# Decode attention beside a gated MLP on one core: three groups of wo behind the last V, a projection in four column tiles, and two K loads left whole

## The chip, the cores and the metric

The kernel runs on one core of one Trainium2 chip. The metric is the device time of that core in microseconds (us). "Span" is the profile's time from the first to the last instruction, some 1.8 us shorter than the device time.

## The reference

Four sequences, one new token each, 32 heads of 128, a cache of 4096 positions. Attention over the cache, a small gated MLP and the residual are summed.

```python
q = (xn @ wq)                                  # (4, 32, 1, 128)
scores = einsum('bhqd,bhkd->bhqk', q, k_cache) * 128 ** -0.5
o = einsum('bhqk,bhkd->bhqd', softmax(scores), v_cache)
attention = o.reshape(4, 1, 4096) @ wo         # wo: (4096, 640)
return x + attention + mlp(xn)                 # xn = layernorm(x)
```

k_cache and v_cache hold 134 MB each in bfloat16; everything else is 14 MB.

## The kernel before

Work is cut into 16 units: four groups of eight heads by four sequences. Each unit has a K and a V of 8.39 MB (64 KB in each of 128 partitions). They are loaded in the order K0 K1 K2 K3 V0 K4 V1 K5 V2 and so on into a ring of five slots; a unit takes two slots, so a load waits until the unit that lay there has been used.

```python
place = {("k", 0): 3, ("k", 1): 0, ("k", 2): 2, ("k", 3): 0}   # first of two slots
for u in range(B, NU):
    place[("k", u)] = 1 if u % 2 == 0 else 0
for u in range(NU):
    place[("v", u)] = 3
...
cuts = {("k", u): (0, T // 2, T) for u in range(B - 1)}        # loads in halves
...
for g in range(NG):
    cuts[("k", B * g + B - 1)] = (0, T // 2, T)
```

For each K unit, VectorE (DVE) transposes eight pieces and TensorE (PE) multiplies them with q. After the fourth unit of a group comes the softmax; then Zb is filled with the probabilities, per sequence, and 64 matmuls with V run in four column tiles (rows 0, 32, 64, 96 of PSUM).

```python
def z_fill(g, b):                       # eight of these on ACT for every V unit
    ... nc.scalar.activation(out=Zb[b % 2][...], in_=src, func=ACT.Copy, scale=MkE[...])

def emit_proj(g, cs=range(HG)):         # 8 chunks, two halves of the 640 columns
    oT = state[("oT", g)]
    for c in cs:
        for hf in range(NH):
            nc.tensor.matmul(proj[32 * hf:32 * hf + B, 0:NO2], lhsT=oT[:, c, :],
                             rhs=wo_t[g][:, c, hf * NO2:(hf + 1) * NO2], ...)
...
emit_proj(NG - 2, range(0, 4))
emit_sel(NG - 1)
emit_proj(NG - 2, range(4, HG))
emit_oT(NG - 1)                         # the attention result of the last group
emit_proj(NG - 1)
o_bf = const.tile([64, NO2], BF16)
nc.vector.tensor_copy(out=o_bf[:], in_=proj[:, 0:NO2])
```

The results of a V unit's four tiles are summed into R. When a group is done, the selection (emit_sel) takes each head's row out of R and divides it by the softmax's sum (om), emit_oT turns the result into oT, and emit_proj multiplies oT with the group's part of wo.

The wo of groups 0 and 1 is loaded in the middle of the stream, that of groups 2 and 3 behind the last V.

Of the kernel before, what the change touches and what calls it, by code (L numbers as in the profile page):

```python
# [8 lines left out]
ACT = mybir.ActivationFunctionType  # L9
ALU = mybir.AluOpType  # L10
AX = mybir.AxisListType
F32 = mybir.dt.float32
BF16 = mybir.dt.bfloat16
# [3 lines left out]
def kernel(  # L17
# [19 lines left out]
    nc = tc.nc  # L37
    P = 128
    B, Sq, D = A_x.shape
# [3 lines left out]
    HG = 8  # L43
    HP = 4
    NE = HG // HP
    M = P // HG
    T = Sk // M
# [4 lines left out]
    NG = H // HG  # L52
    NU = NG * B
# [5 lines left out]
    NOUT = A_wo.shape[1]  # L59
    NH = 2  # L60
    NO2 = NOUT // NH
    scale = float(Dh) ** -0.5
    eps = 1e-5

    const = ctx.enter_context(tc.tile_pool(name="const", bufs=1))
    small = ctx.enter_context(tc.tile_pool(name="small", bufs=2))
# [5 lines left out]
    ps_j = ctx.enter_context(tc.tile_pool(name="ps_j", bufs=1, space=bass.MemoryType.PSUM))  # L72
# [11 lines left out]
    def at_slot(i, n, off=0):  # L84
        return kv[:, i * SL + off:i * SL + off + n]
# [20 lines left out]
    w_out = at_slot(2, FC * NOUT, n_in).rearrange("p (c n) -> p c n", c=FC)  # L106
# [18 lines left out]
        place[("v", u)] = 3  # L125
    place[("v", NU - 3)] = 1
    place[("v", NU - 1)] = 0
    first = {}
    cuts = {("k", u): (0, T // 2, T) for u in range(B - 1)}
    cuts[("v", NU - 1)] = (0, 128, 192, 240, T)  # L130
    for g in range(NG):
        cuts[("k", B * g + B - 1)] = (0, T // 2, T)
    for u in range(B, NU):
        if ("k", u) not in cuts:
            first[u] = u % 2

    def unit(item):
        return at_slot(place[item], 2 * SL)
# [10 lines left out]


    wo_q = A_wo.rearrange("(g p c) n -> g p c n", p=P, c=HG)
    wo_t = [at_slot(3 if g == NG - 2 else 2, HG * NOUT).rearrange("p (c n) -> p c n", c=HG) for g in range(NG)]

    def load_wo(g, c_cuts=(0, HG)):
        for c0, c1 in zip(c_cuts[:-1], c_cuts[1:]):
            nc.sync.dma_start(out=wo_t[g][:, c0:c1, :], in_=wo_q[g][:, c0:c1, :])
# [65 lines left out]
    MkE = const.tile([P, NE], F32)  # L222
# [13 lines left out]
    Zb = []  # L236
# [3 lines left out]
        Zb.append(zt)  # L240


    proj = ps_j.tile([64, 512], F32)



# [1 line left out]
    for hf in range(2):  # L248
        for c in range(DC):
            for j in range(NG):  # L250
                n0 = j * HG * Dh + hf * 512
                nc.tensor.matmul(q4_ps[32 * j:32 * j + 32, hf * 512:hf * 512 + 512], lhsT=xnT[:, c, :],  # L252
                                 rhs=wq[:, c, n0:n0 + 512], start=(c == 0), stop=(c == DC - 1))
# [3 lines left out]
    for r in range(HP):  # L257
        op = nc.vector.tensor_copy if r < 2 else nc.scalar.copy
# [6 lines left out]
    for h in range(HG):  # L265
        for kw in range(4):
            nc.tensor.matmul(q3_ps[:, kw, h, :], lhsT=q4[:, h, kw].rearrange("p r j -> p (r j)"),
                             rhs=SelJ[:].rearrange("p j b -> p (j b)"), start=True, stop=True)
# [5 lines left out]
    for part in range(2):  # L274
        for fc in range(FC):
            n = P if fc < FC - 1 else FL
            f0 = part * Fh
            for c in range(DC):
                if fc < FC - 1:
                    w = w_in[:, c, f0:f0 + nf].rearrange("p (f a) -> p a f", a=FC - 1)[:, fc, :]  # L280
                else:
                    w = w_in[:, c, f0 + nf:f0 + Fh]
                nc.tensor.matmul(zT_ps[:n, part, fc, :], lhsT=w,
                                 rhs=xnT[:, c, 0:B], start=(c == 0), stop=(c == DC - 1))
    zT = const.tile([P, 2, FC, B], F32)
    nc.vector.memset(zT[:], 0.0)
    uT = const.tile([P, FC, 32], BF16)
# [43 lines left out]

    for fc in range(FC):
        n = P if fc < FC - 1 else FL
        nb = B if fc else 32
        for hf in range(NH):
            nc.tensor.matmul(proj[32 * hf:32 * hf + nb, 0:NO2], lhsT=uT[:n, fc, 0:nb],
                             rhs=w_out[:n, fc, hf * NO2:(hf + 1) * NO2], start=(fc == 0), stop=False)


    def fill_qz(g):  # L340
# [50 lines left out]
    def z_fill(g, b):  # L391
        xd = state[("xd", g)]
        for hp in range(HP):
            r0 = 32 * hp
            src = xd[r0:r0 + 32, C2 * b:C2 * b + C2].rearrange("p x q (y c) -> p (x q y) c", c=4)
            for e in range(NE):
                nc.scalar.activation(out=Zb[b % 2][r0:r0 + 32, :, NE * hp + e, :], in_=src, func=ACT.Copy,  # L397
                                     scale=MkE[r0:r0 + 32, e:e + 1])

    def softmax(g):  # L400
        negmax = softmax_max(g)
        S_ps = state.pop(("S", g))
        p_bf = ppool.tile([P, TC, NE, M], BF16, tag="p", name="p")
        rowsum = small.tile([P, NE], F32, tag="rowsum")
        for e in range(NE):
            nc.scalar.activation(out=p_bf[:, :, e, :], in_=S_ps[:, e], func=ACT.Exp, bias=negmax[:, e:e + 1], scale=scale,  # L406
                                 accum_out=rowsum[:, e:e + 1])

        pT = ppool.tile([P, TC, HP, B * C2], BF16, tag="p", name="pT")
        nc.vector.transpose(pT[:].rearrange("p t h x -> p (t h x)"), p_bf[:].rearrange("p t e m -> p (t e m)"))  # L410

        xd = small.tile([P, B * C2, 4, TC], BF16, tag="xd", name="xd", bufs=1)
        state[("xd", g)] = xd
        for hp in range(HP):
            for q in range(4):
                op = nc.vector.tensor_copy if q < 2 else nc.scalar.copy
                op(out=xd[32 * hp:32 * hp + 32, :, q, :], in_=pT[32 * q:32 * q + 32, :, hp, :].rearrange("p t x -> p x t"))  # L417
        z_fill(g, 0)
        z_fill(g, 1)
        cs = misc_ps([G, 1], F32)  # L420
        for e in range(NE):
            nc.tensor.matmul(cs[:], lhsT=SelPe[:, e].rearrange("p h e b -> p (h e b)"), rhs=rowsum[:, e:e + 1],  # L422
                             start=(e == 0), stop=(e == NE - 1))
        rinv = small.tile([G, 1], F32, tag="rinv")
        nc.vector.reciprocal(out=rinv[:], in_=cs[:])
        state[("rinv", g)] = rinv
# [20 lines left out]
    def emit_sel(g):  # L447

        oh = misc_ps([G, Dh], F32)
        for b in range(B):  # L450
            nc.tensor.matmul(oh[:], lhsT=SelR[:, b].rearrange("p h b -> p (h b)"), rhs=state["R"][:, b, :],  # L451
                             start=(b == 0), stop=(b == B - 1))
        om = ppool.tile([G, HG, Dh], BF16, tag="p", name="om")
        nc.vector.scalar_tensor_tensor(out=om[:], in0=oh[:, None, :].to_broadcast((G, HG, Dh)),  # L454
                                       scalar=state.pop(("rinv", g))[:, 0:1],
                                       in1=MkH[:, :, None].to_broadcast((G, HG, Dh)), op0=ALU.mult, op1=ALU.mult)
        state[("om", g)] = om

    def emit_oT(g):
        om = state.pop(("om", g))[:].rearrange("p h (q c) -> p c h q", c=HG)  # L460
        oT_ps = misc_ps([P, HG, B], F32)
        for c in range(HG):
            nc.tensor.matmul(oT_ps[:, c, :], lhsT=om[:, c, :, :], rhs=B32[:], start=True, stop=True)
        oT = small.tile([P, HG, B], BF16, tag="oT")
        nc.vector.tensor_copy(out=oT[:], in_=oT_ps[:])
        state[("oT", g)] = oT

    def emit_proj(g, cs=range(HG)):
        oT = state[("oT", g)]
        for c in cs:  # L470
            for hf in range(NH):
                nc.tensor.matmul(proj[32 * hf:32 * hf + B, 0:NO2], lhsT=oT[:, c, :],  # L472
                                 rhs=wo_t[g][:, c, hf * NO2:(hf + 1) * NO2],
                                 start=False, stop=(g == NG - 1 and c == HG - 1))

    fill_qz(0)
    for i, item in enumerate(seq):
        if i + 1 < len(seq):
            key, u = seq[i + 1]
            if u == NU - 2 and key == "v":  # L480
                nc.sync.dma_start(out=x_res[0:32:4, :], in_=x_flat.rearrange("b (h n) -> (b h) n", h=NH))
            load_unit(seq[i + 1])
            if key == "k" and 2 * B - 1 <= u < NU - 1 and u % B == B - 1:
                load_wo(u // B - 1)
        else:
            load_wo(NG - 2, (0, 4, 8))
            load_wo(NG - 1, (0, 4, 6, 7, 8))
        key, u = item
        g, b = divmod(u, B)
        if key == "k":  # L490
            done = b == B - 1 and g > 0
            for k in range(8):
                emit_K(u, k)
                if done and k == 1:
                    emit_sel(g - 1)
                if done and k == 2:
                    emit_oT(g - 1)
                if done and k == 5 and g < NG - 1:
                    emit_proj(g - 1)
            if b == B - 1:  # L500
                if g < NG - 1:
                    fill_qz(g + 1)
                softmax(g)
        else:
            emit_V(u)
            if u == NU - 2:
                for hf in range(NH):
                    nc.tensor.matmul(proj[32 * hf:32 * hf + B, 0:NO2], lhsT=ident_bf[:32, 4 * hf:32:8], rhs=x_res[:],
                                     start=False, stop=False)
    emit_proj(NG - 2, range(0, 4))  # L510
    emit_sel(NG - 1)
    emit_proj(NG - 2, range(4, HG))
    emit_oT(NG - 1)
    emit_proj(NG - 1)

    o_bf = const.tile([64, NO2], BF16)
    nc.vector.tensor_copy(out=o_bf[:], in_=proj[:, 0:NO2])
    nc.sync.dma_start(out=out_flat[:, 0:NO2], in_=o_bf[0:B, :])
    nc.scalar.dma_start(out=out_flat[:, NO2:NOUT], in_=o_bf[32:32 + B, :])

# [28 lines left out]
```

## Time and profile before

| | before |
|---|---|
| device time, median | 666.86 us (666.03 to 666.89, 6 runs) |
| span of the trace | 665.0 us |
| DVE busy | 353.5 us |
| PE busy | 294.0 us |
| K, V and weights read | 282.25 MB |
| last landing of wo, issue of the output | 660.29, 662.43 us |

The prediction shows the page's shares and slices and the chain over the tail. Two lines of the order of DMA issues follow, and the two landings behind them. The first column is the start in us, the second the length; square brackets give the idle time before the group and what ended it.

```profile
111.56 0.33 SPq L148 DMA_DIRECT2D kv<-in_A_k_cache_dram  x1
133.49 0.33 SPq L148 DMA_DIRECT2D kv<-in_A_v_cache_dram  x1
```

These are K4 and V1. From the same timeline of the kernel before, DVE's first work on K4, and PE's work on V0 and V1:

```profile
141.37 17.66 DVE L356 STREAM_TRANSPOSE kT<-kv 128x2048 f32<-128x2048 f32 x8 [6.37 <-DMA kv<-in_A_k_cache_dram]
...
128.35 5.09 PE L434 MATMUL O<-kv,Zb 128*32 128x512 bf16 x64 [9.77 <-ACT Zb L397]
...
160.74 3.64 PE L434 MATMUL O<-kv,Zb 128*32 128x512 bf16 x64 [0.53 <-DMA kv<-in_A_v_cache_dram]
```

K4 is transposed from 141.37, V1 multiplied from 160.74, and both waited for a DMA: their starts tell when the loads landed. One unit of 8.39 MB lies between them, 19.4 us.

### The profile page before, as it was taken

To read this page: it belongs to the slowest core of one execution; us is meant where nothing else is said; L and a number is where in the kernel's file an instruction comes from. 1 tells how busy PE (TensorE), PEld (TensorE's weight loads), DVE (VectorE), ACT (ScalarE), POOL (GpSimd) and SP (SyncE) were. 2 spreads that over 40 slices of the span, in tenths; PEclk is the share of its full clock that TensorE was granted. 3 is DMA by queue.
4 is the path that set the end of the run, shared out by engine and by line. 5 is a ranking of instruction groups with operands and counts; after the bars stand their busy time and mean duration, and the time that the engine had idled before them with its cause. 6 is when DMAs were issued, how large, how long until landed. Compare 5 with 4: busy or idle time off the path is not lost.

```text
span 665.0 us, 5565 instructions
## 1 busy us (share of the span) xinstructions
PE 294.0 (44%) x2366; PEld 111.6 (17%) x2366; DVE 353.5 (53%) x319; ACT 91.3 (14%) x189; POOL 6.2 (1%) x24
## 2 busy tenths in 40 slices
PE   0566655336052546235335155532705344524365
PEld 0321211112011122011112022210201112111122
DVE  5389997256180849409155286734619074950002
ACT  0300000821100000540200000081020000045200
POOL 0000000000000000000000000000000000000000
PEclk9988788569597697668859596866868769766665
DMA  9999999999999999999999999999999999999995
GB/s 372 424 440 425 426 441 444 438 431 439 434 418 439 434 413 455 434 427 438 419 434 439 434 418 421 452 442 434 427 426 431 438 439 412 464 418 423 429 415 219
DMA packets 7812, 282.60 MB, mean 425 GB/s; under 512 B 888, under 2 KB 1260, under 8 KB 2028
## 3 DMA queue, kind: packets, MB, share of 16 engines
q1 hardware_dynamic: 7772, 282.25, 98.6%
q8 instruction: 18, 0.29, 0.2%
q14 instruction: 6, 0.05, 0.0%
q10 hardware_dynamic: 16, 0.01, 0.0%
HBM read 282.25 MB, written 0.01 MB: 424 GB/s over the span
## 4 chain that ended last, share of the span: by engine, by line
DMA 74%; DVE 10%; issue 10%; PE 3%; ACT 2%; DVEq 0%; SPq 0%; ACTq 0%
DMA kv<-in_A_k_cache_dram 65%; DVE kT L356 9%; DMA kv<-in_A_v_cache_dram 4%; DMA kv<-in_A_wo_dram 3%; DMA kv<-in_A_wq_dram 2%; PE O L434 1%; PE q L252 1%; ACT xd L417 1%; PE proj L472 1%; ACT Zb L397 0%; DVE kv L260 0%; PE S L367 0%; ACT kv L260 0%; ACT p L406 0%; DVE om L454 0%
## 5 line engine op out<-in xcount | busy, mean ns | idle before, releaser
L356 DVE STREAM_TRANSPOSE kT<-kv 128x2048 f32<-128x2048 f32 x128 | 283.4, 2277 | 125.7 <-DMA kv<-in_A_k_cache_dram 125.7
L367 PE MATMUL S<-kT,QZ 128*32 128x512 bf16 x1024 | 185.7, 495 | 232.2 <-DVE kT L356 232.2
L367 PEld LDWEIGHTS <-QZ 128*32 128x32 bf16 x1024 | 59.9, 110 | 351.7 <-issue 330.1
L434 PE MATMUL O<-kv,Zb 128*32 128x512 bf16 x1024 | 75.2, 457 | 66.2 <-ACT Zb L397 39.1
L441 DVE TENSOR_SCALAR R<-O,Mk 128x128 f32<-128x128 f32 x16 | 5.6, 351 | 138.0 <-PE O L434 138.0
L397 ACT ACTIVATE Zb<-xd,MkE 32x256 bf16<-32x256 bf16 x128 | 57.7, 497 | 106.5 <-PE O L434 105.1
L406 ACT ACTIVATE p<-S,negmax 128x512 bf16<-128x512 f32 x8 | 5.4, 683 | 395.1 <-DVE negmax L388 395.1
L434 PEld LDWEIGHTS <-Zb 128*32 128x32 bf16 x1024 | 32.9, 112 | 106.8 <-issue 52.9
L417 ACT COPY xd<-pT 32x256 bf16<-32x256 bf16 x32 | 19.6, 613 | 5.7 <-DVE pT L410 5.2
L443 DVE SCALAR_TENSOR_TENSOR R<-O,Mk,R 128x128 f32<-128x128 f32 x48 | 16.8, 351 | 1.7
L451 PE MATMUL misc<-R,SelR 128*32 128x128 f32 x32 | 6.6, 290 | 24.4 <-DVE R L443 24.4
L417 DVE COPY xd<-pT 32x256 bf16<-32x256 bf16 x32 | 11.7, 364 | 0.6
L472 PE MATMUL proj<-kv,oT 128*4 128x320 bf16 x64 | 9.2, 456 | 1.2 <-DMA kv<-in_A_wo_dram 1.0
L343 POOL COPY QZ<-q 32x32 bf16<-32x32 bf16 x16 | 5.1, 318 | 421.9 <-PE S L367 394.9
L410 DVE STREAM_TRANSPOSE pT<-p 128x1024 bf16<-128x1024 bf16 x4 | 5.0, 1245 | 6.3 <-ACT p L406 6.3
L374 DVE TENSOR_REDUCE m<-S 128x2 f32<-128x1024 f32 x4 | 4.9, 1225 | 5.9 <-PE S L367 5.9
L451 PEld LDWEIGHTS misc<-R,SelR 128*32 128x32 f32 x32 | 2.4, 111 | 31.6 <-DVE R L443 22.7
L260 DVE CAST kv<-q 128x512 bf16<-128x512 f32 x4 | 2.5, 682 | 9.4 <-PE q L252 9.4
L252 PE MATMUL q<-kv,xnT 128*32 128x512 bf16 x40 | 4.5, 629 | 5.1 <-DMA kv<-in_A_wq_dram 5.1
L379 PE MATMUL misc<-dg,ones_f 128*128 128x256 f32 x8 | 3.2, 487 | 7.6 <-DVE dg L376 7.6
L454 DVE SCALAR_TENSOR_TENSOR om<-misc,rinv,MkH 32x1024 bf16<-32x1024 f32 x4 | 5.1, 1272 | 2.6 <-PE misc L451 2.6
L422 PE MATMUL misc<-rowsum,SelPe 128*32 128x1 f32 x16 | 2.1, 200 | 9.0 <-ACT p L406 9.0
(92 smaller groups left out, 60.7 us busy)
## 6 DMA issues: line engine op xcount, KB each, us to landing
kv<-in_A_k_cache_dram SPq DMA_DIRECT2D x14, 4096.0 KB, 30.8
kv<-in_A_wq_dram SPq DMA_DIRECT2D x1, 5120.0 KB, 15.4
kv<-in_A_v_cache_dram SPq DMA_DIRECT2D x1, 4096.0 KB
kv<-in_A_wo_dram SPq DMA_DIRECT2D x2, 1280.0 KB
kv<-in_B_w_in_dram SPq DMA_DIRECT2D x1, 2160.0 KB
kv<-in_A_v_cache_dram SPq DMA_DIRECT2D x1, 2048.0 KB, 33.3
kv<-in_A_wo_dram SPq DMA_DIRECT2D x3, 640.0 KB, 20.0
kv<-in_A_v_cache_dram SPq DMA_DIRECT2D x1, 1536.0 KB
```

The lines of the kernel that those rows point to most:

```text
L252: nc.tensor.matmul(q4_ps[32 * j:32 * j + 32, hf * 512:hf * 512 + 512], lhsT=xnT[:, c, :], rhs=wq[:, c, n0:n0 + 512], start=(c == 0), stop= ...
L343: nc.gpsimd.tensor_copy(out=QZ[r0:r0 + 32, :, :, :, 8 + 8 * hp], in_=q3[r0:r0 + 32, :, NE * hp:NE * hp + NE, g * B:g * B + B].rearrange("p ...
L356: nc.vector.transpose(kT[:].rearrange("p (t r) -> p t r", r=32), kw)
L367: nc.tensor.matmul(S_ps[32 * q:32 * q + 32, e], lhsT=QZ[:, b, 2 * kh + w, e, w0:w0 + 32], rhs=kb[:, i, :, e, :, w], start=(b == 0 and k < ...
L397: nc.scalar.activation(out=Zb[b % 2][r0:r0 + 32, :, NE * hp + e, :], in_=src, func=ACT.Copy, scale=MkE[r0:r0 + 32, e:e + 1])
L406: nc.scalar.activation(out=p_bf[:, :, e, :], in_=S_ps[:, e], func=ACT.Exp, bias=negmax[:, e:e + 1], scale=scale, accum_out=rowsum[:, e:e + 1])
L417: op(out=xd[32 * hp:32 * hp + 32, :, q, :], in_=pT[32 * q:32 * q + 32, :, hp, :].rearrange("p t x -> p x t"))
L434: nc.tensor.matmul(O_ps[32 * q:32 * q + 32, :, :], lhsT=Zb[b % 2][:, w].rearrange("p h c -> p (h c)"), rhs=vv[:, w * 4 * Dh:(w + 1) * 4 * ...
L441: nc.vector.tensor_scalar(out=R, in0=O_ps[:, 0, :], scalar1=Mk4[:, 0:1], scalar2=None, op0=ALU.mult)
L443: nc.vector.scalar_tensor_tensor(out=R, in0=O_ps[:, c, :], scalar=Mk4[:, c:c + 1], in1=R, op0=ALU.mult, op1=ALU.add)
L451: nc.tensor.matmul(oh[:], lhsT=SelR[:, b].rearrange("p h b -> p (h b)"), rhs=state["R"][:, b, :], start=(b == 0), stop=(b == B - 1))
L472: nc.tensor.matmul(proj[32 * hf:32 * hf + B, 0:NO2], lhsT=oT[:, c, :], rhs=wo_t[g][:, c, hf * NO2:(hf + 1) * NO2], start=False, stop=(g == ...
```

## The change

Its intent: let the projections of three groups cover the last group's softmax tail, halve the time of each by using all four column tiles, and save the small cost of cutting two K loads. Some scaling moves from ACT to DVE so that the first V is consumed earlier. The core of the diff:

```diff
-    first = {}
-    cuts = {("k", u): (0, T // 2, T) for u in range(B - 1)}
+    cuts = {("k", u): (0, T // 2, T) for u in range(NU) if u == 1 or u % B == B - 1}
     cuts[("v", NU - 1)] = (0, 128, 192, 240, T)
... (the lines for the other units say the same in another form)
+    first = {u: u % 2 for u in range(B, NU) if ("k", u) not in cuts}
+    first[2] = 1                                   # second half of K2 used first
...
-    wo_t = [at_slot(3 if g == NG - 2 else 2, ...) ...]
+    wo_t = [at_slot((2, 4, 3, 2)[g], ...) ...]
...
-    proj = ps_j.tile([64, 512], F32)
+    proj = ps_j.tile([P, 512], F32)
... (the MLP's chunks go to rows 0 and 64 in turn)
+                if b == 0 and e == 0:              # z_fill: 4 of 8 for the first V
+                    nc.vector.tensor_scalar(out=dst, in0=src, scalar1=mk, ...)
...
-                op = nc.vector.tensor_copy if q < 2 else nc.scalar.copy
+                op = nc.vector.tensor_copy if q < 2 or (hp == 0 and q == 2) else nc.scalar.copy
...
-                nc.tensor.matmul(proj[32 * hf:32 * hf + B, 0:NO2], lhsT=oT[:, c, :],
+                odd = c % 2 == 1 and not (g == NG - 1 and c == HG - 1)
+                r0 = 64 * odd + 32 * hf
+                nc.tensor.matmul(proj[r0:r0 + B, 0:NO2], lhsT=oT[:, c, :],
...
-            load_wo(NG - 2, (0, 4, 8))
+            load_wo(NG - 3)
+            load_wo(NG - 2)
             load_wo(NG - 1, (0, 4, 6, 7, 8))
...
+    emit_proj(NG - 3)
+    emit_sel(NG - 1)
     emit_proj(NG - 2, range(0, 4))
-    emit_sel(NG - 1)
+    emit_oT(NG - 1)
     emit_proj(NG - 2, range(4, HG))
-    emit_oT(NG - 1)
-    emit_proj(NG - 1)
+    emit_proj(NG - 1, range(0, HG - 2))
+    o_1 = const.tile([64, NO2], F32)
+    nc.vector.tensor_copy(out=o_1[:], in_=proj[64:128, 0:NO2])
+    emit_proj(NG - 1, range(HG - 2, HG))
-    nc.vector.tensor_copy(out=o_bf[:], in_=proj[:, 0:NO2])
+    nc.vector.tensor_tensor(out=o_bf[:], in0=proj[0:64, 0:NO2], in1=o_1[:], op=ALU.add)
```

More of the change, by code (lines that the diff above doesn't have):

```diff
@@ L127 @@
     place[("v", NU - 1)] = 0
-    first = {}
-    cuts = {("k", u): (0, T // 2, T) for u in range(B - 1)}
+    cuts = {("k", u): (0, T // 2, T) for u in range(NU) if u == 1 or u % B == B - 1}
     cuts[("v", NU - 1)] = (0, 128, 192, 240, T)
-    for g in range(NG):
-        cuts[("k", B * g + B - 1)] = (0, T // 2, T)
-    for u in range(B, NU):
-        if ("k", u) not in cuts:
-            first[u] = u % 2
+    first = {u: u % 2 for u in range(B, NU) if ("k", u) not in cuts}
+    first[2] = 1
     def unit(item):
@@ L151 @@
     wo_q = A_wo.rearrange("(g p c) n -> g p c n", p=P, c=HG)
-    wo_t = [at_slot(3 if g == NG - 2 else 2, HG * NOUT).rearrange("p (c n) -> p c n", c=HG) for g in range(NG)]
+    wo_t = [at_slot((2, 4, 3, 2)[g], HG * NOUT).rearrange("p (c n) -> p c n", c=HG) for g in range(NG)]
     def load_wo(g, c_cuts=(0, HG)):
@@ L333 @@
         n = P if fc < FC - 1 else FL
-        nb = B if fc else 32
+        nb = B if fc > 1 else 32
+        r0 = 64 * (fc % 2)
         for hf in range(NH):
-            nc.tensor.matmul(proj[32 * hf:32 * hf + nb, 0:NO2], lhsT=uT[:n, fc, 0:nb],
-                             rhs=w_out[:n, fc, hf * NO2:(hf + 1) * NO2], start=(fc == 0), stop=False)
+            nc.tensor.matmul(proj[r0 + 32 * hf:r0 + 32 * hf + nb, 0:NO2], lhsT=uT[:n, fc, 0:nb],
+                             rhs=w_out[:n, fc, hf * NO2:(hf + 1) * NO2], start=(fc < 2), stop=False)
     def fill_qz(g):
@@ L396, in z_fill @@
             for e in range(NE):
-                nc.scalar.activation(out=Zb[b % 2][r0:r0 + 32, :, NE * hp + e, :], in_=src, func=ACT.Copy,
-                                     scale=MkE[r0:r0 + 32, e:e + 1])
+                dst = Zb[b % 2][r0:r0 + 32, :, NE * hp + e, :]
+                mk = MkE[r0:r0 + 32, e:e + 1]
+                if b == 0 and e == 0:
+                    nc.vector.tensor_scalar(out=dst, in0=src, scalar1=mk, scalar2=None, op0=ALU.mult)
+                else:
+                    nc.scalar.activation(out=dst, in_=src, func=ACT.Copy, scale=mk)
     def softmax(g):
@@ L463, in emit_oT @@
             nc.tensor.matmul(oT_ps[:, c, :], lhsT=om[:, c, :, :], rhs=B32[:], start=True, stop=True)
-        oT = small.tile([P, HG, B], BF16, tag="oT")
+        oT = small.tile([P, HG, B], BF16, tag="oT", bufs=3)
         nc.vector.tensor_copy(out=oT[:], in_=oT_ps[:])
@@ L471, in emit_proj @@
             for hf in range(NH):
-                nc.tensor.matmul(proj[32 * hf:32 * hf + B, 0:NO2], lhsT=oT[:, c, :],
+                odd = c % 2 == 1 and not (g == NG - 1 and c == HG - 1)
+                r0 = 64 * odd + 32 * hf
+                nc.tensor.matmul(proj[r0:r0 + B, 0:NO2], lhsT=oT[:, c, :],
                                  rhs=wo_t[g][:, c, hf * NO2:(hf + 1) * NO2],
-                                 start=False, stop=(g == NG - 1 and c == HG - 1))
+                                 start=False, stop=(g == NG - 1 and c in (HG - 3, HG - 1)))
     fill_qz(0)
@@ L482 @@
             load_unit(seq[i + 1])
-            if key == "k" and 2 * B - 1 <= u < NU - 1 and u % B == B - 1:
+            if key == "k" and u == 2 * B - 1:
                 load_wo(u // B - 1)
         else:
-            load_wo(NG - 2, (0, 4, 8))
+            load_wo(NG - 3)
+            load_wo(NG - 2)
             load_wo(NG - 1, (0, 4, 6, 7, 8))
@@ L497 @@
                     emit_oT(g - 1)
-                if done and k == 5 and g < NG - 1:
+                if done and k == 5 and g == 1:
                     emit_proj(g - 1)
```

## The prediction

> **What bounds the kernel now.** I read the page's shares first, then its forty slices, then the chain that ended last, then the stretches of the tail one by one, and last the order of DMA issues. The page of before:
>
> ```profile
> span 665.0 us, 5565 instructions
> PE 294.0 (44%) x2366; PEld 111.6 (17%) x2366; DVE 353.5 (53%) x319; ACT 91.3 (14%) x189; POOL 6.2 (1%) x24
> DMA  9999999999999999999999999999999999999995
> GB/s 372 424 440 425 426 441 444 438 431 439 434 418 439 434 413 455 434 427 438 419 434 439 434 418 421 452 442 434 427 426 431 438 439 412 464 418 423 429 415 219
> DMA 74%; DVE 10%; issue 10%; PE 3%; ACT 2%; DVEq 0%; SPq 0%; ACTq 0%
> ```
>
> No compute engine is busy for much more than half of the span (DVE 53%). The DMA engines are at 90% or more in every slice but the last, at about 430 GB/s. In the packet records a 65,536-byte packet takes 2.42 us, which for 16 engines is 433 GB/s; at least 16 packets are in flight for some 652 of the 665 us. So the kernel is a stream of 282 MB, and the end is set by: the start of the stream, holes in it, its length, and what runs after the last byte. The change removes no bytes, so only holes and the tail can move. The tail, as stretches:
>
> ```profile
> 0.00:640.00 640.00, 279.73 (x2250) 106.07 (x2254) 348.76 (x308) 91.35 (x189) 6.18 (x24) 0.74 1.00 431
> 640.00:655.60 15.60, 8.61 (x82) 2.96 (x75) 2.20 (x7) 0.00 (x0) 0.00 (x0) 0.61 0.98 404
> 655.60:660.30 4.70, 4.12 (x32) 2.10 (x33) 2.07 (x4) 0.00 (x0) 0.00 (x0) 0.50 0.39 153
> 660.30:665.00 4.70, 1.57 (x12) 0.53 (x8) 0.48 (x1) 0.00 (x0) 0.00 (x0) 0.50 0.00 1
> ```
>
> The columns are the stretch, its length, the busy time of PE, PE's weight loads, DVE, ACT and POOL, the granted clock, the DMA share and GB/s. The stream ends at 660.3 and 4.7 us follow without DMA. The completions of the last wo pieces, engine by engine, run from 655.6 to 660.29 in the trace: the fast DMA engines end early, the slowest sets the end. The chain of before over these last microseconds:
>
> ```profile
> 635.57 20.03 DMA kv<-in_A_wo_dram
> ...
> 655.64 1.23 PE proj L472 x8
> 656.87 0.43 PE misc L451 x2
> ...
> 657.33 1.28 DVE om L454
> ...
> 658.65 0.66 PE misc L463 x8
> ...
> 659.33 0.20 DVE oT L465
> ...
> 659.58 2.32 PE proj L472 x16
> ...
> 661.92 0.48 DVE o_bf L517
> ```
>
> The last group's attention result (oT) is ready at 659.53. Only then can its 16 projection matmuls start, 2.32 us of work, although half of the group's wo had landed already. They end at 661.90, 1.6 us after the last byte.
>
> **What the Trainium skill says.** "DMA: Bandwidth & Descriptors", Where 436 GB/s comes from, gives a ceiling of 435.2 GB/s for a core's 16 ports. The trace agrees: 431 GB/s over 640 us, so the rate has no room. The same page, Why a DMA increments its semaphore by 16 and not by 1, says that each engine adds its own count and only all 16 mean landed. The trace agrees: counts of the last pieces spread over 4.7 us, so an engine that idles early costs nothing if the slowest does not idle. "TensorEngine Tiling (Array Packing)", Key Properties, says that different tiles can run their weight loads and matmuls in parallel. The trace agrees: on four column tiles the 64 PV matmuls of 512 columns take 6.11 us, 95 ns each at half clock, while on two column tiles 16 matmuls of only 320 columns take 2.32 us, 145 ns each.
>
> **The change, part by part.**
>
> *wo of group 1 behind the last V.* 1.31 MB at 433 GB/s is 3.0 us. It leaves the queue at 391 us, so V and K from there on land 3.0 us earlier; the stream's length is the same. The last V piece now lands at 651.0 (counts of before: 654.01). PV ends at about 651.7, R at 653.2 (1.5 us, as 654.73 to 656.24 before). wo 1 lands at 654.0, wo 2 at 657.1, wo 3 in pieces at about 658.7, 659.5, 659.9 and 660.3, as before. PE works in this order: projection of wo 1 from 654.0, some 1.2 us on four tiles; the last selection 0.6, to 655.8; om 1.28, to 657.1; half of wo 2; oT matmuls 0.66 and cast 0.2, ready at about 658.5, against 659.53; the other half of wo 2 until 659.0; the first four chunks of wo 3 to 659.5; the next two to 659.8. So TensorE waits for wo and not wo for oT. After the last landing only one chunk is left: two matmuls in different column tiles, 0.47 us each from start to end, side by side.
>
> *Four column tiles and the sum.* They shorten a projection of 16 matmuls from 2.3 to an estimated 1.1 to 1.2 us (320 of 512 columns at 95 ns is 59 ns, plus the filling). The sum costs a copy of the odd half (64x320, 0.48 us like the present cast), which lies beside the last two chunks from 659.85 to 660.35. The final add takes the place of the cast: about 0.5 us for 0.48.
>
> *Whole K loads for units 0 and 2.* In the packet records 65,536 bytes take 2421 ns and twice 32,768 take 2432, and each engine has 8 rows: 0.09 us less per unit. The wo 2 load in one piece: 389 against twice 199 ns, 0.07 us. Together about 0.25 us off the stream. The price is a late start of the transposes. Before:
>
> ```profile
> 34.53 8.89 DVE L356 STREAM_TRANSPOSE kT<-kv 128x2048 f32<-128x2048 f32 x4 [1.56 <-DMA kv<-in_A_k_cache_dram]
> 44.34 8.89 DVE L356 STREAM_TRANSPOSE kT<-kv 128x2048 f32<-128x2048 f32 x4 [0.93 <-DMA kv<-in_A_k_cache_dram]
> 102.64 8.89 DVE L356 STREAM_TRANSPOSE kT<-kv 128x2048 f32<-128x2048 f32 x4 [0.83 <-DMA kv<-in_A_k_cache_dram]
> ```
>
> DVE follows half a unit behind the stream: 8.89 us of transposes for every 9.72 us of landing. After, unit 0 starts at 44.3 and takes 17.8 us, to 62.1; unit 1 to 79.9; unit 2 lands at 83.2 and ends at 101.0; unit 3 ends at 118.8, not 111.5. The fifth K reuses that space, so its issue moves from 111.56 to 118.8, while the V ahead of it finishes landing at 121.87. Then the first softmax begins 7.3 us later.
>
> *Scaling and copying moved from ACT to DVE.* Before, ACT runs 8 copies (5.02 us) and 8 fills (3.7 us) before the first PV. After, 7 copies (4.4) and 4 fills (1.85), while DVE does 9 copies and 4 fills in about 5 us: 2.4 us less from transposes to PV. So the first PV ends at 133.4 + 7.3 - 2.4, about 138.3, and the second V is issued there; the K ahead of it lands at 141.35. First packets move about 1 us after an issue (first issue 0.73, packets within 1.5 to 2.0), so both queues are still just fed: 3 us of slack less 1 us for the start, and the slowest engine counts. From there on the fifth K's own landing sets the rhythm, as before. At the other end, the last softmax also gains 2.4 us, but V's issue at 606.92 was already 8 us ahead of the end of the V in flight (which I put at 615.0, the 634.39 of the next V's landing less 19.4 for 8.39 MB), so that is hidden.
>
> *Sum.* Stream end 660.3 - 0.25 = 660.05; last two matmuls 0.5; add 0.5 with its gaps; output issued at 661.1 against 662.43. That is 1.3 us less. Against 666.78 that gives 665.5; I put 665.4, because the estimate of the last chunk is generous.
>
> **Rivals.** *A hole at 120 or 139 us.* For it: the slack there falls from about 10 and 8 us to 3 each, and TensorE's half clock could lengthen PV by 1.2 us (6.28 against 5.09). Against it: the spread of the engines and the first-packet time of 1 us. If both holes open, up to 1.5 us comes back: 666.3 to 667. *The tail stays bound by oT.* If the order on TensorE puts all of wo 1 and half of wo 2 ahead of the last selection, oT waits for 657.1 and comes at about 660.0; then the last group's matmuls run after it on four tiles, 1.2 us, and the gain is about 0.7 us: 666.1. *The gain goes deeper.* If moving wo out of the middle closes holes there, the time could fall by 3 us, to 663.8; but the slices show no hole there, and the large packets' median rate is already at 433. *A large loss* would need DVE to fall behind the stream for good; it has 17.8 us of transposes per K, and in the steady state 38.7 us of stream per K and V.
>
> **Range and chances.** Three runs of before lie within 0.9 us. The parts that I can size give -0.7 to -1.6, holes give back 0 to 1.5. So 665.4, with 664.3 to 666.9 for 8 in 10. 2% is 13 us; nothing that I found is worth half of that. Faster 0.01, same 0.97, slower 0.02.
>
> **What would show it.** Right: DMA busy to about 660 with the same 431 GB/s; the last wo's landing, not oT, in front of the last projection in the chain; the fifth K issued at about 119 and the second V at about 138, with no slice near them below 400 GB/s; 3.6 us from the last landing to the end of the span (0.5 and 0.5 and the 2.6 from the output's issue, 662.43 to 665.0 before), not 4.7. Wrong: an idle stretch of DMA at 120 or 139 us, oT later than 659.5, or a stream rate that differs by over 0.3%, which would be 2 us and outweigh everything above.

## The result, and the profile after

The changed kernel takes 667.83 us (median of 6 runs, 666.70 to 668.32) against 666.86. The ratio is 1.0013, with a 95% interval of 1.0000 to 1.0026. A ratio here is the mean time of one kernel's fast runs over that of the other's of the same rounds, so it is not quite the ratio of the medians. The class "within 2%" was right; the time lies 0.9 us above the top of the predicted range, and the predicted small gain came out as a small loss. From the page of the changed kernel:

```profile
span 666.5 us, 5583 instructions
GB/s 374 452 409 462 413 425 438 440 371 440 434 440 438 433 410 444 425 438 437 434 440 425 430 421 441 425 438 440 434 437 426 429 437 416 451 437 426 412 417 224
```

The ninth slice, from 133 to 150 us, moved 371 GB/s; before it was 431. The order of issues and the landings of the changed kernel, for the lines shown of before:

```profile
118.17 0.33 SPq L144 DMA_DIRECT2D kv<-in_A_k_cache_dram  x1
139.06 0.33 SPq L144 DMA_DIRECT2D kv<-in_A_v_cache_dram  x1
...
82.94 35.20 DVE L353 STREAM_TRANSPOSE kT<-kv 128x2048 f32<-128x2048 f32 x16 [3.68 <-DMA kv<-in_A_k_cache_dram]
...
141.89 17.66 DVE L353 STREAM_TRANSPOSE kT<-kv 128x2048 f32<-128x2048 f32 x8 [1.31 <-DMA kv<-in_A_k_cache_dram]
...
132.80 6.21 PE L435 MATMUL O<-kv,Zb 128*32 128x512 bf16 x64 [7.57 <-ACT Zb L399]
...
163.01 3.64 PE L435 MATMUL O<-kv,Zb 128*32 128x512 bf16 x64 [2.29 <-DMA kv<-in_A_v_cache_dram]
```

K2 lands at 82.9 as a whole, and K2 and K3 then take 35.2 us of transposes without a pause, to 118.14. K4, which reuses a slot of K3 (and one of K2), is issued there, 6.6 us later than before. It lands 0.5 us later. V1 is issued when V0 has been used, at 139.06, and lands 2.3 us later than before. That delay stays to the end: the last wo lands at 662.64 instead of 660.29. The stretches around the issue of V1, the kernel before first (columns as in the prediction; the last two are the DMA share and GB/s):

```profile
136.00:140.00 4.00, 0.00 (x0) 0.00 (x0) 0.00 (x0) 1.21 (x3) 0.00 (x0) 0.77 0.99 426
140.00:144.00 4.00, 0.26 (x2) 0.13 (x3) 2.63 (x2) 0.00 (x0) 0.00 (x0) 0.50 1.02 442
144.00:148.00 4.00, 3.52 (x16) 0.95 (x13) 4.00 (x3) 0.00 (x0) 0.00 (x0) 0.50 0.91 393
```

and the changed kernel:

```profile
136.00:140.00 4.00, 3.01 (x36) 1.00 (x28) 0.86 (x3) 1.38 (x4) 0.00 (x0) 0.74 0.62 266
140.00:144.00 4.00, 0.38 (x2) 0.23 (x3) 2.66 (x3) 2.71 (x6) 0.00 (x0) 0.68 1.29 475
144.00:148.00 4.00, 3.44 (x16) 1.09 (x16) 4.00 (x3) 0.00 (x0) 0.00 (x0) 0.50 0.72 311
```

A packet counts with the stretch in which it starts, so single shares swing by a tenth or more; but 266, 475 and 311 sum to 4.2 MB, against 5.0 MB for 426, 442 and 393. The packet records show why. A DMA engine ends each of its loads with a packet of 4 bytes that counts up the semaphore. The 16 engines end K4 between 138.97 and 140.68. The first packets of V1 start at 140.01, 0.95 us after the issue; 13 engines start by 140.51 and the last three at 141.55 to 142.01. And these first packets take 2.70 to 3.69 us, not 2.42. The same happens at K4's issue: the engines end V0 from 119.20 on, K4's first packet starts at 119.21, and eleven of K4's first packets take 2.57 to 3.04 us. So there are two holes (stretches in which DMA engines idle because the next load is issued late), one at K4's issue and one at V1's. How much the first one costs differs between traces: in this one the last engine ends K4 at 140.70, no later than before (140.85), and K4 is used late only because the last of its 16 counts came 1.19 us after the last packet (paired in order, the other fifteen counts came 0.3 to 0.5 us after theirs); in the second trace of the same kernel, below, the engines end K4 as late as 142.80.

The tail of the changed kernel, from the timeline (the third and fourth columns are engine and line):

```profile
658.34 0.19 DVE L466 CAST oT<-misc 128x32 bf16<-128x32 f32 x1 [0.77 <-PE misc L464]
659.53 1.24 PE L476 MATMUL proj<-kv,oT 128*4 128x320 bf16 x16 [1.23 <-DMA kv<-in_A_wo_dram]
661.07 1.26 PE L476 MATMUL proj<-kv,oT 128*4 128x320 bf16 x12 [0.30 <-DMA kv<-in_A_wo_dram]
662.38 0.49 DVE L522 COPY o<-proj 64x320 f32<-64x320 f32 x1 [3.85 <-PE proj L476]
662.92 0.70 PE L476 MATMUL proj<-kv,oT 128*4 128x320 bf16 x4 [0.60 <-DVE o L522]
663.66 0.48 DVE L526 TENSOR_TENSOR o_bf<-proj,o 64x320 bf16<-64x320 f32 x1 [0.79 <-PE proj L476]
664.17 0.30 SPq L527 DMA_DIRECT2D out_dram<-o_bf  x1
```

oT is ready more than a microsecond before the last projections, which wait for wo: as intended. But the last four matmuls waited for the copy of the odd half ("DVE o"), though they write other rows. From the last landing to the output's issue it takes 1.53 us, 2.14 before, and not the 1.05 of the prediction.

The sums of the two traces: last landing +2.35, landing to issue of the output -0.61, issue to the end -0.16 (2.54 and 2.38); together +1.58, which is the difference of the spans (664.97 and 666.55).

### The profile page after: what moved, and what is told of

Same layout as the page of the kernel before. It is cut to its first block, busy times and chain, and to the rows that moved or that the text cites. A ratio compares the mean times of both kernels' runs of the same rounds, so it can differ in the third digit from the quotient of the medians.

```text
span 666.5 us, 5583 instructions
## 1 busy us (share of the span) xinstructions
PE 298.7 (45%) x2366; PEld 110.7 (17%) x2366; DVE 359.2 (54%) x340; ACT 82.7 (12%) x169; POOL 6.2 (1%) x24
## 4 chain that ended last, share of the span: by engine, by line
DMA 72%; DVE 12%; issue 12%; PE 2%; ACT 1%; SPq 1%; DVEq 0%; ACTq 0%
DMA kv<-in_A_k_cache_dram 64%; DVE kT L353 11%; DMA kv<-in_A_v_cache_dram 4%; DMA kv<-in_A_wo_dram 3%; PE O L435 2%; DVE xd L418 0%; ACT Zb L399 0%; PE S L364 0%; ACT p L407 0%; DVE pT L411 0%; DVE m L371 0%; SPq L152 0%; PE proj L476 0%; SPq L110 0%; PE misc L376 0%
## 5 line engine op out<-in xcount | busy, mean ns | idle before, releaser
L364 PE MATMUL S<-kT,QZ 128*32 128x512 bf16 x1024 | 191.2, 507 | 231.2 <-DVE kT L353 231.2
L435 PE MATMUL O<-kv,Zb 128*32 128x512 bf16 x1024 | 77.3, 467 | 62.0 <-ACT Zb L399 30.3
L399 ACT ACTIVATE Zb<-xd,MkE 32x256 bf16<-32x256 bf16 x112 | 51.5, 499 | 107.2 <-PE O L435 105.8
L418 ACT COPY xd<-pT 32x256 bf16<-32x256 bf16 x28 | 17.2, 614 | 5.7 <-DVE pT L411 5.2
L418 DVE COPY xd<-pT 32x256 bf16<-32x256 bf16 x36 | 13.1, 364 | 0.6
L476 PE MATMUL proj<-kv,oT 128*4 128x320 bf16 x64 | 6.9, 453 | 2.5 <-DMA kv<-in_A_wo_dram 1.7
```

Of the source, the lines that this page charges most:

```text
L364: nc.tensor.matmul(S_ps[32 * q:32 * q + 32, e], lhsT=QZ[:, b, 2 * kh + w, e, w0:w0 + 32], rhs=kb[:, i, :, e, :, w], start=(b == 0 and k < ...
L399: nc.scalar.activation(out=dst, in_=src, func=ACT.Copy, scale=mk)
L418: op(out=xd[32 * hp:32 * hp + 32, :, q, :], in_=pT[32 * q:32 * q + 32, :, hp, :].rearrange("p t x -> p x t"))
L435: nc.tensor.matmul(O_ps[32 * q:32 * q + 32, :, :], lhsT=Zb[b % 2][:, w].rearrange("p h c -> p (h c)"), rhs=vv[:, w * 4 * Dh:(w + 1) * 4 * ...
L476: nc.tensor.matmul(proj[r0:r0 + B, 0:NO2], lhsT=oT[:, c, :], rhs=wo_t[g][:, c, hf * NO2:(hf + 1) * NO2], start=False, stop=(g == NG - 1 an ...
```

## The experiments

My theory had two parts. First, the late issues of K4 and V1, both caused by the whole load of K2, open the holes. Second, the copy stands in front of the last matmuls because both halves lie in one PSUM tile. Rivals: the loss comes from the three wo groups or the extra DVE work; the late start with the whole K0 is the cause; large loads are slow in themselves. All kernels in the table but the first two rows ran with five rounds beside the kernel before; the two single looks told further down are of unknown state, as one run cannot tell.

| run | time, median (lowest to highest) | ratio to before, 95% interval | K4 used from | V1 used from | last landing | landing to output |
|---|---|---|---|---|---|---|
| before | 666.86 (666.03 to 666.89) | | 141.37 | 160.74 | 660.29 | 2.14 |
| changed | 667.83 (666.70 to 668.32) | 1.0013 (1.0000 to 1.0026) | 141.89 | 163.01 | 662.64 | 1.53 |
| e1 | 665.97 (665.88 to 666.17) | 0.9991 (0.9979 to 1.0003) | 141.36 | 160.73 | 660.16 | 1.51 |
| e2 | 666.14 (665.70 to 666.15) | 0.9991 (0.9979 to 1.0003) | 141.12 | 160.50 | 659.98 | 1.49 |
| e3 | 666.83 (665.76 to 668.27) | 1.0006 (0.9994 to 1.0018) | 142.14 | 161.60 | 660.92 | 1.49 |
| e4 | 665.46 (665.41 to 665.59) | 0.9984 (0.9972 to 0.9996) | 141.25 | 160.63 | 660.27 | 1.03 |
| e5 | 666.82 (666.58 to 667.29) | 1.0005 (0.9993 to 1.0018) | 142.59 | 162.34 | 661.63 | 1.03 |
| e6 | 668.89 (666.88 to 669.08) | 1.0029 (1.0016 to 1.0043) | 142.48 | 163.02 | 662.59 | 2.13 |
| e7 | 666.32 (665.46 to 666.54) | 0.9994 (0.9980 to 1.0007) | 141.39 | 160.76 | 660.34 | 1.88 |
| e8 | 665.80 (665.67 to 665.98) | 0.9991 (0.9977 to 1.0004) | 141.21 | 160.57 | 660.27 | 1.09 |
| e9 | 667.60 (665.88 to 668.05) | 1.0013 (1.0000 to 1.0026) | 141.92 | 161.36 | 660.14 | 1.50 |
| e10 | 666.25 (666.08 to 666.53) | 0.9996 (0.9984 to 1.0009) | | | 660.41 | 1.51 |

The last four columns are from each run's one trace, in us; for e9 the first part of V1 was used earlier, and the column gives the wait for the whole of it; in e6 DVE came to K4 only at 142.48 and did not wait for it, as it had landed at 141.03. In e10 both loads are used in parts. The kernel before had medians of 666.65 (e1 to e4), 666.77 (e5, e6, e7, e9) and 666.75 (e8, e10). All results were correct.

**e1: K loads in halves again.**

```diff
-    cuts = {... for u in range(NU) if u == 1 or u % B == B - 1}
+    cuts = {... for u in range(NU) if u < B or u % B == B - 1}
-    first[2] = 1
```

> The changed kernel with the K loads of units 0 and 2 in halves again. Theory (whole K loads open holes in the DMA stream): the fifth K is issued at about 111.5 again, the second V at about 131, no hole, the last DMA lands at 660.0 to 660.4 instead of 661.85, and the time falls by about 2 us to 665.7 to 666.3, that is level with or 0.5 below the kernel before. Rival (the loss comes from three groups of wo at the end, or from the DVE work): the time stays at 667.5 to 668.

Measured 665.97, as the theory says. (The 661.85 of the expectation was the landing of an earlier piece; the changed kernel's last is 662.64.) The issues of K4 and V1 are back at 111.47 and 132.46, and no stretch between 20 and 640 us has fewer than 16 packets in flight. So wo at the end and the extra work on DVE don't cost the stream anything. Of the changed kernel's time, 1.9 us (667.83 less 665.97) are due to the two whole K loads. In this trace the first PV took 6.53 us, longer than in the changed kernel, and it did no harm.

**e2: only K0 whole.**

```diff
-    cuts = {... if u == 1 or u % B == B - 1}
+    cuts = {... if u in (1, 2) or u % B == B - 1}
-    first[2] = 1
```

> The changed kernel with K unit 0 whole and K unit 2 in halves. Theory (unit 2 is the one that matters, since its landing at 83 us holds the transposes up and those of unit 0 have caught up by then only in part): transposes of unit 3 end at about 115.5, fifth K issued there, second V at about 136; both are some 3 us before the first DMA engine runs dry, so hardly a hole: time 665.8 to 666.7. Rival (the late start of unit 0 is the cause): as slow as the changed kernel, 667.5 to 668.

Measured 666.14, within the theory's range and outside the rival's. K4 was issued at 114.32 and V1 at 135.08. The loads ahead landed at 121.61 and 141.1, some 7 and 6 us after those issues, and only 0.01 us of hole is left (time between 20 and 640 us with fewer than 16 packets in flight, all queues counted, weighted by the share that is missing; the changed kernel has 0.97). K4 lands 0.24 us sooner than in e1. That this is the saving of the whole load is not shown: V0, which is behind the same loads, lands between 121.55 and 121.90 in the nine traces with whole K loads and between 121.78 and 121.95 in the five with halves, so one pair of traces is within the scatter.

**e3: only K2 whole.**

```diff
-    cuts = {... if u == 1 or u % B == B - 1}
+    cuts = {... if u in (0, 1) or u % B == B - 1}
```

> The changed kernel with K unit 0 in halves and K unit 2 whole. Theory (unit 2 alone sets the end of unit 3's transposes: 83.2 + 35.2 = 118.4): the fifth K issued at 118 and the second V at 138 to 139 as in the changed kernel, the same holes, 667.2 to 668. Rival (unit 0 is the cause): 665.8 to 666.5.

Measured 666.83, between the two ranges, and with the widest spread of all. The K4 issue at 118.25 is as expected, and the first hole is there: K4 is used 0.78 us later than in e1. But V1 was issued at 137.58, not 138 to 139, because the first PV took 5.07 us here and not 6.21, and the second hole hardly opened. V1 was used from 161.60, 0.87 us later than in e1, which is the first hole alone. So K2 opens the first hole by itself, and in this trace the short first PV kept the second one shut. The timed runs reach from no loss at all to as much as the changed kernel's, so the median expected was too high.

**e4: halves again, and the odd half of the projection in a PSUM tile of its own.**

```diff
-    proj = ps_j.tile([P, 512], F32)
+    proj_e = ps_j.tile([P, 512], F32, tag="pe", name="proj_e")
+    proj_o = ps_j.tile([P, 512], F32, tag="po", name="proj_o")
...
+                pr = proj_o if odd else proj_e
-                nc.tensor.matmul(proj[r0:r0 + B, 0:NO2], ...
+                nc.tensor.matmul(pr[r0:r0 + B, 0:NO2], ...
... (the MLP's chunks, the residual, the copy and the add likewise; K loads as in e1)
```

> As e1, and the odd halves of the projection have a PSUM tile (bank) of their own. Theory (in the changed kernel the last two chunks waited for the copy of the odd half because both halves lie in one tile): the copy runs beside the last two chunks, the output is issued 1.1 to 1.4 us after the last landing instead of 2.3, and the time is 0.8 to 1.2 us below e1, at 664.8 to 665.4. Rival (the copy sits in front because the last wo pieces land late, not because of the tile): same as e1 within 0.3 us.

```profile
659.91 0.83 PE L478 MATMUL proj_e<-kv,oT 128*4 128x320 bf16 x4
...
659.97 0.49 DVE L524 COPY o<-proj_o 64x320 f32<-64x320 f32 x1 [3.83 <-PE proj_o L478]
...
660.78 0.48 DVE L528 TENSOR_TENSOR o_bf<-proj_e,o 64x320 bf16<-64x320 f32 x1 [0.32 <-PE proj_e L478]
661.29 0.30 SPq L529 DMA_DIRECT2D out_dram<-o_bf  x1
```

The copy now runs beside the last four matmuls, and the output is issued 1.03 us after the last landing. The theory holds; the gain over e1 is 0.51 us, less than the 0.8 to 1.2 I expected, because e1's tail was already 1.51 and not the 2.3 on which that expectation rested (I had at first taken an earlier piece's landing for the last). At 665.46 this is the fastest of all kernels tried, and better than both: 0.16% under the kernel before by the ratio, 2.4 us under the changed one by the medians.

**e5: the changed kernel with only the PSUM tile of its own** (e4's edit of the PSUM tiles on the changed kernel).

> The changed kernel with the K loads as changed (0 and 2 whole) and only the odd halves of the projection in a PSUM tile of their own. Theory (holes and the wait for the copy are two separate costs): the holes stay, so the last landing stays 0.5 to 2 us later than in e1, depending on the clock in the first PV; the copy no longer stands in front of the last two chunks, output issued 0.5 to 1 us sooner after the last landing than in the changed kernel. Time 666.0 to 667.4. Rival (one bank cured both): 665.5 as e4.

Measured 666.82, inside the theory's range and outside the rival's. Both holes are there (V1 used from 162.34), and from landing to output it takes 1.03 us. The two costs are separate.

**e6: the kernel before with nothing but the whole K0 and K2** (the change's lines on cuts and first alone).

> The kernel before with nothing of the change but K units 0 and 2 whole. Theory (without the four scalings and the copy moved to DVE the first PV ends 2.3 us later): the fifth K issued at 118.2 and the second V at 140 to 141.5, that is 1.5 to 2.5 us later than in the changed kernel, so the second hole is larger; time 668.5 to 670.5. Rival (whole K loads cost nothing by themselves): 666.4 to 666.9.

Measured 668.89, in the theory's range: whole K loads alone make the kernel before 2.1 us slower. The reason that I gave for the number is only half right. V1 was issued at 141.04 as expected and the hole is larger to the eye:

```profile
136.00:140.00 4.00, 4.00 (x48) 1.51 (x40) 0.00 (x0) 2.59 (x6) 0.00 (x0) 0.52 0.63 266
140.00:144.00 4.00, 1.37 (x22) 0.51 (x15) 2.84 (x5) 2.81 (x7) 0.00 (x0) 0.91 0.78 262
```

But V1 landed at 163.0, just as in the changed kernel, whose V1 was issued 2 us sooner. There, 13 engines started V1 by 140.51 and three only at 141.55 to 142.01; here all 16 started at 142.01 to 142.66. The engine that ends its first packet last sets the landing, and it did so at 145.70 there and at 145.73 here. So in these two traces the work moved from ACT to DVE bought nothing for the stream, and the difference of about 1 us to the changed kernel is the older tail (2.13 against 1.53) and the spread.

**e7: the kernel before with nothing but the wo of group 1 moved behind the last V.**

```diff
-            load_wo(NG - 2, (0, 4, 8))
+            load_wo(NG - 3)
+            load_wo(NG - 2)
...
+    emit_proj(NG - 3)
+    emit_sel(NG - 1)
     emit_proj(NG - 2, range(0, 4))
-    emit_sel(NG - 1)
+    emit_oT(NG - 1)
     emit_proj(NG - 2, range(4, HG))
-    emit_oT(NG - 1)
     emit_proj(NG - 1)
... (the slots of wo and the buffers of oT as in the change)
```

> The kernel before with nothing of the change but the wo of group 1 loaded after the last V and projected at the end, still in two column tiles. Theory (TensorE then has 3 projections of 2.3 us behind the last V on two tiles, of which the last ends later than before): oT ready sooner but the last projection held up by the ones ahead; time 666.5 to 667.5. Rival (moving wo out of the middle frees the stream): 664 to 665.5.

Measured 666.32, 0.2 below the theory's range and far above the rival's; the interval against before includes 1. The last landing is where it was (660.34), and the tail 1.88 us instead of 2.14. Moving wo frees nothing in the stream, and with two column tiles it also buys little at the end: the last 32 matmuls run without a pause for 4.43 us, from 657.24.

**e8: the kernel before with nothing but the four column tiles**, each half in its own PSUM tile, and the sum.

> The kernel before with nothing of the change but the four column tiles, each half in a PSUM tile of its own, and the halves added at the end; wo and K loads as before. Theory (oT stays ready at 659.5, the last group's 16 matmuls then take 1.2 instead of 2.3 us, the add costs no more than the cast): output issued 0.9 to 1.1 us sooner than before, time 665.6 to 666.1. Rival (the tail is set by the last landing and not by these matmuls): 666.4 to 666.9.

Measured 665.80, as expected. The output is issued at 661.36 instead of 662.43, with the same last landing (660.27). So the four column tiles with their own PSUM tiles bring about 1.0 us by themselves. The other parts of e4 come to 0.3 us more by the medians; with the tails 0.06 us apart and the same last landing, that gain is not shown.

**e9: the changed kernel with V1 loaded in two halves.**

```diff
+    cuts[("v", 1)] = (0, T // 2, T)
```

> The changed kernel, with the load of the second V unit in two halves, so that its first half can be issued when the first half of the first V has been consumed, some 3 us sooner. Theory (the second hole comes from the issue of that V at 139, and costs 1.75 us when PV runs at half clock): the first half issued at about 136, no hole at 139, the first hole at 118 stays at 0.8 us: time 666.0 to 667.0 and a narrower spread than the changed kernel's 666.7 to 668.3. Rival (the loss is in the K loads themselves, not in the lead of the issue): 667.5 to 668.3.

The trace is as the theory says: V1's first half was issued at 136.52, K4 is 0.8 us late as in the changed kernel, and the wait for all of V1 ended at 161.36, that is, the second hole is gone. The times are not: 665.88 in the profiled run, but 667.31 to 668.05 in the other four, so the expectation of 666.0 to 667.0 with a narrower spread failed.

> The kernel of e9 once more, for a trace: its five timed runs lay between 665.88 and 668.05 and the trace was of the fastest. Theory (what varies is the first hole and the tail): if this run is slow, the fifth K lands later than 142.5 or the tail after the last landing is longer than 2 us. Rival: the second V lands later than 162, so that its halves did not close the second hole.

That run took 666.86. K4 was used from 142.00, V1 completely from 161.44, the last landing came at 661.15 and the tail took 1.49. Again the second hole was closed, and neither the theory's reason nor the rival's for a slow run shows up, as this run wasn't slow. The two traces show one more source of spread, which no late issue explains: V1 lands within 0.1 us of the same time in both, but the last landing is 1.0 us apart. Nearly all of it arises at the second piece of the last V, which landed 5.87 us after the first piece here and 4.90 in e9's trace, though all pieces had been issued by 616.2; one engine's count came 1 us after the other fifteen. What made the four runs slow stays open; no trace of them was kept.

**The changed kernel once more.**

> The changed kernel once more, for a trace, to see how the two holes vary from run to run: fifth K landing 0.7 to 1.5 us later than the 141.1 without holes, second V 0.8 to 2.6 us later than 160.5, the time above 665.9 by about what the second V is late.

Measured 668.23. K4 was used from 143.13, 2.0 us later than the 141.12 of e2, more than expected; V1 from 162.90, 2.4 later than the 160.50 of e2. The 665.9 of the expectation plus 2.4 would be 668.3. So the first hole varies too: K4 was used 0.8 to 2.0 us late in the traces with a late issue, and in e6 it wasn't late at all. The two don't simply add; an engine that started late at the first may have less to lose at the second, which is argued and not shown.

**e10: the K loads stay whole, but the loads behind the holes are issued sooner.**

```diff
+    cuts[("v", 1)] = cuts[("k", 4)] = cuts[("k", 5)] = (0, T // 2, T)
-    first[2] = 1
+    first[2] = first[4] = 1
... (K4's second half, whose slot is free sooner, is loaded first)
+    for t0, t1 in list(zip(c[:-1], c[1:]))[::-1 if item == ("k", 4) else 1]:
```

> The changed kernel with K units 0 and 2 still whole, but the three loads behind the holes issued sooner: the fifth K in halves, the half whose space is free first loaded and transposed first (issue near 101 instead of 118), the second V in halves (near 136 instead of 138 to 139) and the sixth K in halves. Theory (the loss is the late issue, not the size of the K loads): no idle stretch of DMA between 110 and 150, last landing at 660.0 to 660.5, time 665.7 to 666.4 and a spread under 0.6, as with split K loads. Rival (whole K loads cost in themselves, or the extra DVE work does): 667 to 668 as the changed kernel.

The order of issues in its trace, first for the two halves of K4, then for those of V1:

```profile
100.84 17.87 SPq L145 DMA_DIRECT2D kv<-in_A_k_cache_dram  x2
137.17 3.15 SPq L145 DMA_DIRECT2D kv<-in_A_v_cache_dram  x2
```

K4's first part is issued at 100.84, V1's at 137.17. Measured 666.25 with a spread of 0.45, and 0.04 us of hole. The transposes end as late as in the changed kernel (DVE's softmax work begins at 120.12, 119.38 there) and the first PV took 6.42 us, longer than there. So neither the size of the K loads nor the late transposes nor the slow PV cost anything by themselves, to within the 0.3 us to e1's median; the late issue of the loads behind them does. Against e9, which closed only the second hole and took 667.60, this run closes the first as well. So in most of the timed runs the larger part of the loss probably went with the first hole, although the trace shown above has it at V1; this run also has the sixth K in halves, so the two runs don't prove it.

## Why the prediction was wrong

**What bounds the kernel** was right: DMA, end to end, with only holes and the tail to win or lose. e7 confirms that moving wo frees nothing in the stream.

**"Both queues are still just fed"** is the step that failed. The issue of K4 was predicted at 118.8 and came at 118.17; that of V1 at 138.3 and 139.06. Those terms were good, in part by luck: PV took 1.1 us longer than assumed, and transposes that ended 0.6 us sooner than assumed hid half of that. The lead that I held against them was mis-sized in three ways. I measured the slack to the landing of the load ahead, 121.87 and 141.35, which is when the slowest engine's count arrives. The first engine runs dry about 2.3 us sooner: 119.20 and 138.97 in the changed kernel's records, where V0 landed at 121.61 and K4 was used from 141.89. I took 1 us from issue to first packet, which is right for the first engine (1.04 and 0.95; at K4 that engine was busy until then); the last one started V1 2.95 us after the issue. And I took it that only the slowest engine counts. But the packets that restart together took 2.6 to 3.7 us instead of 2.42, at V1 on all 16 engines, and that held the slowest up too. The rival "a hole at 120 or 139 us" had the right places and the right causes, half clock included, with at most 1.5 us; the two traces of the changed kernel show V1 2.2 to 2.3 us later than in the kernel before.

**PV at 5.1 us** was one trace's value. It took 5.07 to 6.53 us over the traces here. The Trainium skill, "TensorE: Matmul & The Clock Gate", Part 1: The HAM clock gate, gives two states, half and full clock, switched by a free-running window of about 3.4 us, and warns that the same kernel varies from run to run. The clock records of all 14 traces agree: the granted clock is 0.5 or 1.0, and it changes only on a grid of 3.413 us. The first PV takes, within 0.06 us in every trace, 3.64 us (as the PV of V1 at full clock in the kernel before) plus half of the time that it spends at half clock: with 2.98 us of half clock it took 5.09 in the kernel before, with 5.25 it took 6.21 in the changed one, with 5.91 it took 6.53 in e1. So the spread is that of the moment at which the clock rises. A slack that is smaller than this spread is no slack. For the same reason the prediction's "95 ns each at half clock" is a mean over both clocks: that PV began its groups of four matmuls every 0.43 us until the clock rose at 605.78 and every 0.22 us after, 107 and 54 ns each. The comparison with 145 ns on two tiles stands, and 16 projection matmuls on four tiles took 1.24 us for the estimated 1.1 to 1.2.

**The tail.** oT was to be ready at 658.5 and early enough; in e4, without holes, it came at 655.95 to 656.14, because the last selection ran ahead of the projection of wo 1 (653.25 and 654.08), although kernel.py writes the two in the other order. That it would no longer be waited for was right. "After the last landing only one chunk is left" was wrong by 0.5 us: the copy of the odd half held the last four matmuls, since both halves lie in one tile. With a tile of its own the tail took 1.03 us, and the prediction had 1.05.

**The whole loads.** The 0.09 us per unit was neither confirmed nor refuted: e2 has K4 0.24 us sooner than e1 with one unit whole, which is within the scatter of the landings, and nothing of it is visible in the device times.

**The sum.** Predicted from 665.0 to about 663.7 in the span. e4, with the queue fed and the tail freed, has 663.8. Two steps were missing: the holes, 2.35 us at the last landing with whatever the whole loads save already taken off, and the tile, 0.5.

## What to carry to other kernels

When a kernel is bound by DMA, the thing to protect is the lead of each issue. Take it from the moment at which the first engine finishes the load ahead, allow some 3 us for all engines to start (2.95 in the changed kernel's trace, 1.62 in e6's), and add the spread of whatever releases the buffer; a saving of a tenth of a microsecond is not worth using up that lead. And when two halves of a result are to be drained at different times, give each a PSUM tile of its own; in this program the drain of one held up the writes to the other by 0.5 us.

## What the Trainium skill lacked or had wrong

- "DMA: Bandwidth & Descriptors", Specifications, gives a first-byte latency of about 0.6 us for loads issued from SP. V1's first packet started 0.95 us after the start of its issue in the changed kernel and 0.97 in e6; counted from the end of the 0.33 us that the issue takes, that is 0.62 and 0.64, which agrees. What the page lacks is how late the sixteenth engine starts: up to 2.95 us after the issue (V1 of the changed kernel; 1.62 in e6, where all engines were idle).
- The same page does not say that packets that start together after a dry spell are slow. The first ones of 65,536 bytes took 2.57 to 3.69 us on eleven engines at K4 and on all 16 at V1 of the changed kernel, against a median of 2.42. In the kernel before, 15 of 3072 such packets took over 2.7 us, all scattered; in the changed kernel 43 of 3328 did, 25 of them between 119 and 142.1 us.
- The same page explains that a semaphore counts 16 engines, but not how far apart they finish in a long stream: 1.8 us at V0's landing of the kernel before (120.1 to 121.87), 4.8 us at V14's (629.6 to 634.39).
- "PSUM — Partial Sum Buffer", in its rules for kernel authors, does advise a different bank for reading while matmuls run; what it lacks is the price of not doing so. Here it cost 0.5 us (e5 against the changed kernel, e4 against e1). It is the program's own wait: in the trace the matmul at 662.92 waits for a semaphore that the copy counts up. Whether the chip would need it was not tried.
